# A spectral layer and a mixture of experts on one core: a prefix product in another PSUM ring, bias products over 128 rows, opening loads in another order, and one test for three tiles

## The chip, the cores and the metric

The kernel runs as one program on one core of one Trainium2 chip. The metric is device time in microseconds (us), from one execution of the whole program; a measurement is the median of some such executions. In the profile, PE is TensorE (PEld its weight loads), DVE is VectorE, ACT is ScalarE, POOL is GpSimd, and SP is the engine whose queue issues most DMAs. A "q" behind an engine's name (SPq, POOLq) means its sequencer.

## The reference

Eight sequences of 2496 tokens with 256 channels go through a spectral layer, and all 19968 tokens of its output through a mixture of eight experts, of which each token uses one:

```python
X = np.fft.rfft(x, axis=1)                       # x: (8, 2496, 256)
Yr = Xr @ w_r - Xi @ w_i + b_r
Yi = Xr @ w_i + Xi @ w_r + b_i
Y = soft_threshold(Yr, 0.01) + 1j * soft_threshold(Yi, 0.01)
y = np.fft.irfft(Y, n=2496, axis=1).reshape(19968, 256)

expert = argmax(y @ w_gate, axis=1)              # 8 experts
gate = softmax(y @ w_gate)[expert]
out = gate * (relu(y @ w1[expert]) @ w2[expert]) # 256 -> 1024 -> 256
```

## The kernel before

**The spectral part.** The transform of 2496 = 39 x 64 points is done in two stages of matmuls. For a batch `b`, `fwd_a` multiplies 39-point pieces of `x` (product `pa`), and the result goes to DRAM (`spec_dram<-ae`, or `spec_dram<-z` for the first batch). `turn(b, s)` reads it back in another order (`t<-spec_dram`, two DMAs for each step `s` of ten), and `fwd_b` does the 64-point stage with a table `bm` (product `pb`). `halves` splits the result into high and low parts for exact products on DVE and ACT. `mix` multiplies by the weights (products `pk` and `pm`; `pk` is read into `k`, then `pm` and `k` are added to `u`, in the profile `v`), `shrink` is the soft threshold (`y`), and `inv_b` (product `pv`, table `bi`) and `inv_a` (products `pz` and `py`, result `yb`) transform back. One loop of 80 iterations `it`, ten for each batch, holds all of this: iteration `it` does `fwd_b` of the next step, `mix` of its own, `shrink` of the one before and `inv_b` of the one before that, and places pieces of `fwd_a` of a later batch and of `inv_a` of an earlier one by lists of offsets. For the last batch the two halves of `pm` begin with a product of the tiles `ones` and `bias_r`, which adds `b_r` and `b_i` (row 0 of `bias_r` holds the rounded bias, row 32 what rounding left; both tiles have 33 rows).

**PSUM.** The accumulators lie in small rings of banks. Pool `psi` has a ring `u` of four banks (`pa`, `pv`, `pz`, the experts' `po`, some of the first iteration's) and a ring `yo` of two banks (`py`, and small products of routing and of the tables). Pool `psf` has one bank `b` (`pb`) and one bank `m` (`pk`, then `pm`); a product that takes a bank waits until its last tenant has been read.

**Routing.** For each half batch `route` finds the expert of every token and its place among that expert's rows. The places need a prefix sum over 117 partitions, which is the small product `pr` (lines 668 to 670, two matmuls), read by DVE into `rb`. POOL then scatters the rows into `xs_dram`. `route` and `table` are generators: `tick(n)` lets the oldest of them take `n` steps, each a small DVE operation or two, between the other work. `write_blank` fills eight blank tiles of `xs_dram` by eight DMAs from POOL.

**The experts.** Tiles of 256 rows are multiplied with `w1` (`ph`, line 949; ACT makes `hh`, DVE `hl`) and `w2` (`po`, lines 983 to 986); POOL scatters the results to `out`. `table(0)` and `table(1)` compute which expert and rows each tile has. `finish_last` runs `table(1)` beside the first seven tiles; it ends with the products `pq` and `pl`, whose input `lap` DVE writes. 85 tiles are possible; `experts_rest` runs tiles 7 to 81 always, and 82 to 84 each under a test (`tc.If`) of a count `live`. With these inputs none of the three is run.

The order on PE, SP, ACT and DVE is the order in which the code is written; on SP, DMAs stand in one queue.

Of the kernel before, what the change touches and what calls it, by code (L numbers as in the profile page):

```python
# [24 lines left out]
D = 256  # L25
# [75 lines left out]
class Kernel:  # L101
# [71 lines left out]
    def open_forward(self, st):  # L173
# [18 lines left out]
        self.bias_r = f.tile([33, 2, D], F32R, name="bias_r")  # L192
        self.ones = f.tile([33, 128], F32R, name="ones")
# [67 lines left out]
    def split_bias(self, part):  # L261
        nc = self.nc
        if part == 0:
            nc.scalar.activation(self.bias_r[0:32], self.bias[0:32], AF.Copy, scale=self.tcol[0:32, 2:3])
        elif part == 1:
            bh = self.w.tile([33, 2, D], F32R, tag="y", name="bh", bufs=3)
            nc.scalar.copy(bh[32:33], self.bias[32:33])
            nc.vector.tensor_sub(self.bias_r[32:33], self.bias[32:33], bh[32:33])
        else:
            nc.scalar.activation(self.ones, self.ident[0:33], AF.Copy, scale=0.0, bias=1.0)  # L270
# [75 lines left out]
    def mix(self, b, s):  # L346
# [25 lines left out]
        if b or s:  # L372
            p = self.psf.tile([128, 2, D], F32, tag="m", name="pm", bufs=1)
        else:
            p = self.psi.tile([128, 512], F32, tag="u", name="pm", bufs=4).rearrange("p (a d) -> p a d", a=2)
# [67 lines left out]
    def spectral(self, fwd):  # L443
# [7 lines left out]
        for i, pair in enumerate(pairs):  # L451
            self.fwd_a(0, *pair)
            if i == 4:
                self.load_basis("bm", 0, 2)
                self.load_w("r")
            if i == 6:
                self.load_w("i")
                for h, v in ((0, self.b_r), (1, self.b_i)):
                    self.nc.sync.dma_start(self.brow[:, h, :], bass.AP(v.tensor, v.offset, [[D, 1], [1, D]]))
        self.turn(0, 0)  # L460
        self.turn(0, 1)
        self.load_basis("bm", 2, 6)
        self.turn(0, 2)
        if nb > 1:
            self.load_x(1, 0)
        self.turn(0, 3)
        self.load_basis("bi", 0, 4)
# [9 lines left out]
        for b in range(1, nb):  # L477
            at = 10 * b - 10
            for i, o in enumerate((1, 2, 2, 3, 3, 4, 4, 5, 5, 6, 6) if b == 1 else (-3, -2, -1, 0, 0, 1, 2, 3, 4, 5, 6)):
                first[at + o].append((b, *pairs[i]))  # L480
            for q, o in enumerate((None, 0, 1, 2, 3, 4) if b == 1 else (-7, -5, -4, -2, 0, 2)):
                if o is not None:
                    loads[at + o].append((b, q))
# [9 lines left out]
        for it in range(n):  # L493
# [35 lines left out]
            for a in pieces[it][1:]:  # L529
                self.inv_a(*a)  # L530
            for a in loads[it]:
                self.load_x(*a)
# [4 lines left out]
            if it == 6:  # L537
                self.write_blank(self.us[b, s][0:1, 0, 0:1])
            if it < 4:
                self.load_basis(*(("bm", 6, 12), ("bi", 4, 10), ("bm", 12, 20), ("bi", 10, 20))[it])  # L540
            if it + 4 < n and (it != 6 or nb == 1):
# [48 lines left out]
    def breathe(self):  # L590
        self.tick(3)

    def finish_last(self):
        tiles = itertools.chain.from_iterable(self.step(t) for t in range(BUSY))
        fill = itertools.chain(self.first1(), self.first2())
        for i in range(GH + 1):
# [14 lines left out]
        self.jobs.append(self.table(1))  # L611
        for _ in tiles:
            self.breathe()
# [7 lines left out]
    def route(self, b, hf, y):  # L621
# [46 lines left out]
        p = self.psi.tile([128, 512], F32, tag="yo", name="pr")  # L668
# [36 lines left out]
    def table(self, last):  # L705
# [82 lines left out]
        if last:  # L788
            lap = rt.tile([128, 128], F32, name="lap")
            nc.vector.tensor_copy(lap, fin[:, 3:4].broadcast_to((128, 128)))  # L790
            for _ in range(4):
# [226 lines left out]
    def experts_rest(self, late):  # L1018
        late.enter_context(self.tc.manual_schedule(engines={mybir.EngineType.Activation, mybir.EngineType.DVE}))
        main = self.nt - RARE  # L1020
# [3 lines left out]
        live = self.nc.values_load(self.tabs[1][0:1, 3, 0:1], min_val=0, max_val=self.nt)  # L1024
        nt = self.nt
        for t in range(main, nt):
            with self.tc.If(live > t - self.early):
# [30 lines left out]
```

## Time and profile before

| | |
|---|---|
| median of 3 runs | 1551.67 us (1549.34 to 1552.24) |
| the profiled execution's own time | 1549.26 us |
| its span, first to last instruction | 1547.4 us |
| PE busy | 1512.6 us, 98% of the span |
| DVE, ACT, POOL busy | 62%, 49%, 25% |
| mean granted TensorE clock | 0.995 |

The span falls into an opening (0 to 35 us), the loop of 80 iterations (35 to about 570 us), a stretch in which the last batch is transformed back and the first expert tiles run (to about 670 us), and the experts. A busy PE in these tables includes the time in which a matmul runs through the array behind the next one, so that the steady spacing of starts tells more than the busy time.

### The profile page before, as it was taken

What the parts mean: (1) busy time and instruction counts of PE and PEld (TensorE: products, weight loads), DVE (VectorE), ACT (ScalarE), POOL (GpSimd) and SP (SyncE); (2) the same over time, 40 slices, a digit from 0 to 9 for tenths busy, and PEclk for the clock granted to TensorE, in tenths of its full rate; (3) what the DMA queues carried; (4) which work ended last, traced back from release to release, by engine and by line L of the source; (5) the groups of instructions that cost most, each with busy time, mean ns of one, the idle gap of its engine ahead of it and who ended that gap; (6) DMA issues with size and microseconds to landing.
All of it is one profiled execution on the core that took longest, in us unless ns stands there. A gap on an engine that the chain in (4) does not pass through costs nothing. (4 is left out here: it accounts for less than half of the span.)

```text
span 1547.4 us, 35414 instructions
## 1 busy us (share of the span) xinstructions
PE 1512.6 (98%) x10808; PEld 1383.2 (89%) x10808; DVE 957.2 (62%) x2178; ACT 759.0 (49%) x1629; POOL 392.5 (25%) x550
## 2 busy tenths in 40 slices
PE   8999999999999999999999999999999999999997
PEld 3779899999898889899999999999999999999996
DVE  3778888889898777745555455454545445445442
ACT  2666766767666565434444434343434334334332
POOL 1100243343444453333421111111111111111111
PEclk9999999999999999999999999999999999999999
DMA  7954455555543332434443323232314124132210
GB/s 227 269 177 115 132 169 149 151 165 153 156 143 118 108 78 54 114 90 104 120 115 97 99 53 93 56 94 64 85 42 105 43 50 100 43 82 65 50 42 20
DMA packets 194726, 162.03 MB, mean 105 GB/s; under 512 B 127868, under 2 KB 164516, under 8 KB 194513
## 3 DMA queue, kind: packets, MB, share of 16 engines
q1 hardware_dynamic: 174705, 115.53, 29.2%
q0 software_dynamic: 19808, 44.03, 8.4%
q8 instruction: 88, 1.44, 0.4%
q14 instruction: 125, 1.02, 0.2%
HBM read 241.99 MB, written 66.37 MB: 199 GB/s over the span
## 5 line engine op out<-in xcount | busy, mean ns | idle before, releaser
L986 PE MATMUL po<-h,hh 128*128 128x512 f32 x1312 | 461.9, 395 | 0.0
L949 PE MATMUL ph<-xh,h 128*128 128x256 f32 x1312 | 372.0, 284 | 1.1 <-DVE hl L955 1.0
L949 PE MATMUL ph<-xl,h 128*128 128x256 f32 x1312 | 371.1, 283 | 0.0
L949 PE MATMUL ph<-xh,l 128*128 128x256 f32 x1312 | 370.7, 283 | 0.0
L983 PE MATMUL po<-h,hl 128*128 128x256 f32 x1148 | 323.9, 282 | 0.0
L955 DVE SCALAR_TENSOR_TENSOR hl<-ph,hh 128x512 fp32r<-128x512 f32 x328 | 226.1, 689 | 147.4 <-ACT hh L954 95.0
L954 ACT ACTIVATE hh<-ph 128x512 fp32r<-128x512 f32 x328 | 193.7, 598 | 205.5 <-PE ph L949 197.8
L986 PEld LDWEIGHTS po<-h,hh 128*128 128x128 f32 x1312 | 241.5, 188 | 43.4
L995 POOL DMA_INDIRECT out<-o,row x124 | 123.2, 994 | 581.6 <-DVE o L993 479.0
L993 DVE SCALAR_TENSOR_TENSOR o<-po,xr,part 128x256 f32<-128x256 f32 x156 | 75.4, 484 | 302.3 <-ACTq L911 153.7
L949 PEld LDWEIGHTS ph<-xh,l 128*128 128x128 f32 x1312 | 251.2, 191 | 3.7
L949 PEld LDWEIGHTS ph<-xh,h 128*128 128x128 f32 x1312 | 251.2, 191 | 2.5 <-DVE hl L955 2.1
L949 PEld LDWEIGHTS ph<-xl,h 128*128 128x128 f32 x1312 | 251.2, 191 | 0.0
L992 ACT ACTIVATE part<-po,xr 128x256 f32<-128x256 f32 x156 | 73.8, 473 | 334.5 <-PE po L986 318.3
L983 PEld LDWEIGHTS po<-h,hl 128*128 128x128 f32 x1148 | 215.5, 188 | 6.0 <-DVE hl L955 1.6
L690 POOL DMA_INDIRECT xs_dram<-yb,pos x176 | 179.8, 1021 | 103.5 <-issue 55.8
L392 DVE SCALAR_TENSOR_TENSOR y<-v,r 64x256 f32<-64x256 f32 x320 | 133.4, 417 | 5.0 <-ACT r L386 0.8
L421 PEld LDWEIGHTS pz<-iw,z 128*120 128x120 f32 x704 | 90.7, 183 | 22.2 <-issue 22.1
L421 PE MATMUL pz<-iw,z 128*120 128x136 f32 x704 | 96.7, 280 | 0.0
L409 ACT COPY z<-pv 128x256 f32<-128x256 f32 x160 | 92.7, 700 | 2.1 <-PE pa L293 1.4
L326 PE MATMUL pb<-bm,t 128*128 128x128 f32 x640 | 85.4, 276 | 5.1 <-DMA t<-spec_dram 2.8
L337 ACT COPY re<-pb 128x256 f32<-128x256 f32 x80 | 29.6, 370 | 116.8 <-PE pb L326 102.7
(183 smaller groups left out, 2556.7 us busy)
## 6 DMA issues: line engine op xcount, KB each, us to landing
r<-moe_w SPq DMA_DIRECT2D x672, 128.0 KB
r<-moe_w SPq DMA_DIRECT2D x166, 512.0 KB
xq<-xs_dram SPq DMA_DIRECT2D x332, 64.0 KB
t<-spec_dram SPq DMA_DIRECT2D x160, 128.0 KB
spec_dram<-ae SPq DMA_DIRECT2D x78, 240.0 KB
x<-x SPq DMA_DIRECT2D x40, 384.0 KB
x<-x SPq DMA_DIRECT2D x40, 84.0 KB
xs_dram<-yb,pos POOLq DMA_INDIRECT x176
```

What stands on the lines that cost most here:

```text
L326: nc.tensor.matmul(p[:, c, :, kp, :], t[:, kp, c * 128:(c + 1) * 128], self.bm[:, 2 * s + kp, :], start=True, stop=True)
L392: nc.vector.scalar_tensor_tensor(out=y[q * 64:q * 64 + 64, kp, :], in0=u[h, q, :], scalar=LAM, in1=r[h, q, :], op0=ALU.add, op1=ALU.min)
L409: nc.scalar.copy(self.zs[b % 2][:, c, 0:NB, 4 * s:4 * s + 4].rearrange("p n a -> p a n"), p[:, c].rearrange("p a r n -> p (a r) n"))
L421: nc.tensor.matmul(p[:120, c * 136:(c + 1) * 136], self.zs[b % 2][:, c, 3 * g:3 * g + 3, :].rearrange("p j a -> p (j a)"), self.iw[:, c, : ...
L690: i = nc.gpsimd.indirect_dma_start(out=self.xs[:, :], out_offset=bass.IndirectOffsetOnAxis(ap=pos[:n, g:g + 1], axis=0), in_=y[:n, g, 0:XW ...
L949: nc.tensor.matmul(p[:, i, :], a[:, c, f * 128:(f + 1) * 128], v[:, c, :], start=m == 0, stop=m == 5)
L954: nc.scalar.activation(hh[:, s, :], p, AF.Relu)
L955: nc.vector.scalar_tensor_tensor(out=hl[:, s, :], in0=p, scalar=0.0, in1=hh[:, s, :], op0=ALU.max, op1=ALU.subtract)
L983: nc.tensor.matmul(p[:, :D], hl[:, f - 1, hs], w2[:, f - 1, 0, :], start=False, stop=False)
L986: nc.tensor.matmul(p, hh[:, f, hs], w2[:, f].rearrange("p a d -> p (a d)"), start=f == 0, stop=f == 7)
L993: nc.vector.scalar_tensor_tensor(out=o[:, h, :], in0=p[:, :D], scalar=xr[:, h, 0:1], in1=part, op0=ALU.mult, op1=ALU.add)
L995: i = nc.gpsimd.indirect_dma_start(out=self.out[:, :], out_offset=bass.IndirectOffsetOnAxis(ap=at[h], axis=0), in_=o[:, h, :], in_offset=N ...
```

## The change

Five groups of edits.

- `route`'s product `pr` takes a bank of the ring `u` (four) in place of `yo` (two).
- `ones` and `bias_r` have 128 rows in place of 33, the added rows of `bias_r` being zero; the bias matmuls are over 128 rows.
- The opening loads `bm` 0:4 at once (0:2 before), then 4:8 (2:6 before), and reads `turn(0, 3)` and `bi` ahead of the first `x` of batch 1. In the first iterations each load of `bm` or `bi` stands ahead of the `x` loads of that iteration. `pm` of step 1 takes a bank of `u`, as that of step 0 does, and the first `fwd_a` of batch 1 stands an iteration later. `write_blank` is called in iteration 11 in place of 6.
- While only `table(1)` is left, `breathe` gives it two steps in place of three, and it waits seven steps in place of four between `lap` and `pl`.
- `live` is read ahead of tile 7, and one test stands around the three conditional tiles. In SP's, PE's, ACT's and DVE's order the read moves from behind the last tile to the place ahead of tile 7; on POOL it stays at the end.

```diff
-        self.bias_r = f.tile([33, 2, D], F32R, name="bias_r")
-        self.ones = f.tile([33, 128], F32R, name="ones")
+        self.bias_r = f.tile([128, 2, D], F32R, name="bias_r")
+        self.ones = f.tile([128, 128], F32R, name="ones")
...
-            nc.scalar.activation(self.bias_r[0:32], self.bias[0:32], AF.Copy, scale=self.tcol[0:32, 2:3])
+            nc.scalar.activation(self.bias_r, self.bias, AF.Copy, scale=self.tcol[:, 2:3])
...
-            nc.scalar.activation(self.ones, self.ident[0:33], AF.Copy, scale=0.0, bias=1.0)
+            nc.scalar.activation(self.ones, self.ident, AF.Copy, scale=0.0, bias=1.0)
...
-        if b or s:
+        if b or s > 1:
             p = self.psf.tile([128, 2, D], F32, tag="m", name="pm", bufs=1)
         else:
             p = self.psi.tile([128, 512], F32, tag="u", name="pm", bufs=4).rearrange("p (a d) -> p a d", a=2)
...
-                self.load_basis("bm", 0, 2)
+                self.load_basis("bm", 0, 4)
...
-        self.load_basis("bm", 2, 6)
+        self.load_basis("bm", 4, 8)
         self.turn(0, 2)
+        self.turn(0, 3)
+        self.load_basis("bi", 0, 4)
         if nb > 1:
             self.load_x(1, 0)
-        self.turn(0, 3)
-        self.load_basis("bi", 0, 4)
...
-            for i, o in enumerate((1, 2, 2, 3, 3, 4, 4, 5, 5, 6, 6) if b == 1 else (-3, -2, -1, 0, 0, 1, 2, 3, 4, 5, 6)):
+            for i, o in enumerate((2, 2, 3, 3, 4, 4, 5, 5, 5, 6, 6) if b == 1 else (-3, -2, -1, 0, 0, 1, 2, 3, 4, 5, 6)):
...
+            if it < 4:
+                self.load_basis(*(("bm", 8, 12), ("bi", 4, 10), ("bm", 12, 20), ("bi", 10, 20))[it])
+            if not it:
+                self.turn(*todo[4])
             for a in loads[it]:
                 self.load_x(*a)
...
-            if it == 6:
+            if it == 11:
                 self.write_blank(self.us[b, s][0:1, 0, 0:1])
-            if it < 4:
-                self.load_basis(*(("bm", 6, 12), ("bi", 4, 10), ("bm", 12, 20), ("bi", 10, 20))[it])
-            if it + 4 < n and (it != 6 or nb == 1):
+            if 0 < it < n - 4 and (it != 6 or nb == 1):
...
-        self.tick(3)
+        self.tick(2 if len(self.jobs) == 1 and self.last_table else 3)
...
-        p = self.psi.tile([128, 512], F32, tag="yo", name="pr")
+        p = self.psi.tile([128, 512], F32, tag="u", name="pr", bufs=4)
...
-            for _ in range(4):
+            for _ in range(7):
                 yield
             p = self.psi.tile([128, 512], F32, tag="yo", name="pl")
...
-        main = self.nt - RARE
+        main, nt = self.nt - RARE, self.nt
+        live = self.nc.values_load(self.tabs[1][0:1, 3, 0:1], min_val=0, max_val=nt)
         for t in range(BUSY, main):
             for _ in self.step(t):
                 pass
-        live = self.nc.values_load(self.tabs[1][0:1, 3, 0:1], min_val=0, max_val=self.nt)
-        nt = self.nt
-        for t in range(main, nt):
-            with self.tc.If(live > t - self.early):
+        with self.tc.If(live > main - self.early):
+            for t in range(main, nt):
                 if t > main:
                     self.nt = t
                     self.weights_now(t)
```

On SP's queue, behind the reads `turn(0, 0)` and `turn(0, 1)` of the opening, stood before (`bm<-c_bm 128x512` is 256 KB, `128x768` 384 KB; `x<-x` of 96 rows 384 KB; each `t` 128 KB twice):

```order
L216 DMA bm<-c_bm 128x512
L313 DMA t_243<-spec_dram 64x2x256 x2
L286 DMA x<-x 96x1x1024
L286 DMA x<-x 21x1x1024
L313 DMA t_249<-spec_dram 64x2x256 x2
L216 DMA bi<-c_bi 128x512
L286 DMA x<-x 96x1x1024
L286 DMA x<-x 21x1x1024
L216 DMA bm<-c_bm 128x768
```

And now, at the same place:

```order
L216 DMA bm<-c_bm 128x512
L313 DMA t_243<-spec_dram 64x2x256 x2
L313 DMA t_246<-spec_dram 64x2x256 x2
L216 DMA bi<-c_bi 128x512
L286 DMA x<-x 96x1x1024
L286 DMA x<-x 21x1x1024
L216 DMA bm<-c_bm 128x512
```

The first row was `bm` 2:6 and is now 4:8; `turn(0, 3)` (`t_249` before, `t_246` now) has moved ahead of the first `x` of batch 1; `bm` 6:8, which stood in the last row of before behind two loads of `x`, is now in the first.

On DVE, beside the fourth expert tile that `table(1)` runs along with, stood before, from the tile's first `hl` to its second (the small 128x8 operations are `table(1)`'s):

```order
L955 SCALAR_TENSOR_TENSOR hl<-ph,hh 128x512
L921 STREAM_TRANSPOSE xf<-xq 128x8x2x32
L741 TENSOR_TENSOR st_9430<-pfb,cnt 128x8
L744 TENSOR_TENSOR te<-tcol,pfb 128x8
L746 COPY ge<-te 128x8
L747 TENSOR_REDUCE fin<-te 128x1
L744 TENSOR_TENSOR te<-tcol,pfb 128x8
L747 TENSOR_REDUCE fin<-te 128x1
L749 TENSOR_SCALAR fin<-fin 128x2
L750 TENSOR_TENSOR fin<-fin 128x1
L955 SCALAR_TENSOR_TENSOR hl<-ph,hh 128x512
```

And now, between the same two:

```order
L959 SCALAR_TENSOR_TENSOR hl<-ph,hh 128x512
L925 STREAM_TRANSPOSE xf<-xq 128x8x2x32
L742 TENSOR_TENSOR cnt<-cnt,used 128x8
L718 COPY pfa<-cnt 128x8
L721 COPY pfb<-pfa 128x1
L722 TENSOR_TENSOR pfb<-pfa 128x7
L959 SCALAR_TENSOR_TENSOR hl<-ph,hh 128x512
```

Eight small operations stood between the two, now four, and the rest of the table has moved to later places; `pq` and `pl` stand on PE about a tile later than before.

On POOL, at the end of the program, behind the read of `live` (the row `ISA` is the instruction that, where a tile is skipped, counts up the semaphores of its DMAs; the profile calls it INC_SWDGE_SEM), stood before:

```order
L1027 COMPARE_AND_BRANCH
L911 UNCONDITIONAL_BRANCH
L995 DMA out<-o,row 19968x256 x2
L1027 UNCONDITIONAL_BRANCH
L1027 ISA
L1027 UNCONDITIONAL_BRANCH
L1027 COMPARE_AND_BRANCH
L903 UNCONDITIONAL_BRANCH
L911 UNCONDITIONAL_BRANCH
L995 DMA out<-o,row 19968x256 x2
L1027 UNCONDITIONAL_BRANCH
L1027 ISA
```

and the same once more for the third tile. Now stands there, for all three tiles:

```order
L1029 COMPARE_AND_BRANCH
L915 UNCONDITIONAL_BRANCH
L999 DMA out<-o,row 19968x256 x2
L907 UNCONDITIONAL_BRANCH
L915 UNCONDITIONAL_BRANCH
L999 DMA out<-o,row 19968x256 x2
L907 UNCONDITIONAL_BRANCH
L915 UNCONDITIONAL_BRANCH
L999 DMA out<-o,row 19968x256 x2
L1029 UNCONDITIONAL_BRANCH
L1029 ISA
```

A program that skips the tiles met three compares and three `ISA`, and now meets one of each.

## Rows read from the trace of the kernel before

**Rows 1.** PE's waits over the span: us in total, times, longest.

```profile
PE py L438 <- ACT yb L439: 7.7, 11, 1.3
PE pb L326 <- DMA t<-spec_dram: 2.8, 2, 2.0
```

**Rows 2.** Three stretches: us, each engine's busy us (x instructions), clock, DMA share, GB/s.

```profile
50.00:75.00 25.00, 24.82 (x165) 20.05 (x164) 19.95 (x45) 17.78 (x39) 2.67 (x7) 1.00 0.95 277
100.00:125.00 25.00, 25.00 (x196) 23.02 (x195) 19.92 (x44) 18.05 (x45) 0.00 (x0) 1.00 0.37 106
...
580.60:584.00 3.40, 3.24 (x15) 2.90 (x15) 3.26 (x12) 3.05 (x9) 1.87 (x4) 0.50 0.24 73
```

**Rows 3.** Timeline, 30 to 43 us: start, us, engine, what [idle before <-releaser].

```profile
32.62 1.13 PE L326 MATMUL pb<-bm,t 128*128 128x128 f32 x8 [1.12 <-DMA bm<-c_bm]
...
37.09 0.44 SPq L216 DMA_DIRECT2D bm<-c_bm  x1
...
37.55 1.02 PE L293 MATMUL pa<-x,far 117*120 117x512 f32 x2
...
39.66 0.39 PE L359 MATMUL pm<-whd,sh 128*128 128x256 f32 x1 [1.09 <-DVE k L368]
...
41.72 0.69 DVE L379 TENSOR_TENSOR v<-pm,k 128x512 f32<-128x512 f32 x1
...
42.52 1.13 PE L326 MATMUL pb<-bm,t 128*128 128x128 f32 x8 [1.18 <-DMA spec_dram<-ae]
```

**Rows 4.** Timeline, 73 to 84 us, POOL, SP and PE.

```profile
73.09 4.27 POOL L232 DMA_DIRECT2D xs_dram<-blank  x8 [0.45 <-POOL blank L230]
...
75.71 5.79 SPq L313 DMA_DIRECT2D t<-spec_dram  x4
...
83.55 1.13 PE L326 MATMUL pb<-bm,t 128*128 128x128 f32 x8 [2.04 <-DMA t<-spec_dram]
```

**Rows 5.** Timeline of PE and DVE around three of the products pr.

```profile
190.85 0.20 PE L670 MATMUL pr<-carry_b,ones_b 117*117 117x8 bf16 x1
...
192.16 0.29 PE L438 MATMUL py<-zl,gh 120*117 120x272 f32 x1
192.93 0.39 PE L438 MATMUL py<-zh,gh 120*117 120x272 f32 x1 [0.47 <-ACT yb L439]
...
193.26 0.17 DVE L672 SCALAR_TENSOR_TENSOR rb<-pr,base 117x8 f32<-117x8 f32 x1
193.28 0.29 PE L438 MATMUL py<-zl,gh 120*117 120x272 f32 x1
193.40 0.29 PE L359 MATMUL pm<-whd,sh 128*128 128x256 f32 x1
...
530.08 0.38 PE L438 MATMUL py<-zh,gh 120*117 120x272 f32 x1 [1.18 <-ACT yb L439]
...
590.24 0.38 PE L438 MATMUL py<-zh,gh 120*117 120x272 f32 x1 [0.61 <-ACT yb L439]
```

**Rows 6.** The bias products: the line's group, and PE's timeline around one.

```profile
L355 PE MATMUL pm<-bias_r,ones x20: 378/381/384, 501.7 to 564.8; 33*128 33x256 f32 x20
...
553.17 0.28 PE L359 MATMUL pm<-whd,sl 128*128 128x256 f32 x1
553.38 0.38 PE L355 MATMUL pm<-bias_r,ones 33*128 33x256 f32 x1
553.69 0.39 PE L359 MATMUL pm<-whs,sh 128*128 128x256 f32 x1
```

**Rows 7.** PE's timeline beside the last table.

```profile
637.82 0.39 PE L949 MATMUL ph<-xh,h 128*128 128x256 f32 x1 [0.73 <-DVE hl L955]
...
650.65 0.49 PE L794 MATMUL pl<-ident,lap 128*128 128x128 f32 x2 [1.50 <-DVE lap L790]
```

**Rows 8.** The end on POOL: two lines' groups (ns min/median/max, first and last start).

```profile
L1027 POOLq INC_SWDGE_SEM  x3: 1180/1194/1236, 1538.1 to 1541.0; - x3
...
L1054 POOLq DRAIN  x3: 46/109/4317, 1542.3 to 1547.1; - x3
```

More of the change, by code (lines that the diff above doesn't have):

```diff
@@ L595, in finish_last @@
         fill = itertools.chain(self.first1(), self.first2())
+        self.last_table = False
         for i in range(GH + 1):
@@ L611, in finish_last @@
         self.jobs.append(self.table(1))
+        self.last_table = True
         for _ in tiles:
```

## The prediction

> **What bounds the kernel now.** I read the table first: PE is busy for 98% of the span, at a granted clock of 0.995. So no other engine is a bound over any long stretch, and an edit can gain only where PE stands still, where its matmuls are spaced wider than they need be, or behind its last matmul. Next I read PE's waits. There the reader is to see how little there is: the longest entry is `py` waiting for ACT's copy `yb`, 7.7 us in eleven waits, then `pb` waiting for the reads of `spec_dram`, 2.8 us [rows 1]. The remaining views are timelines at those places, to see what the waiting product's bank or input hangs on, and the stretches, for the DMA load. Between 50 and 75 us the DMA engines are 0.95 busy at 277 GB/s, and 50 us later 0.37 at 106 GB/s [rows 2]. Waits alone don't tell all: the twenty bias products cause hardly a wait but break the spacing of matmuls [rows 6], and the end of the program has no PE in it at all [rows 8].
>
> **The change part by part.** All sums are against the profiled execution's own 1549.26 us.
>
> *Opening loads and `pm` of step 1.* The larger first load puts 128 KB more into a saturated queue ahead of everything that the first `pb` needs: at 277 GB/s [rows 2] that is 0.47 us lost. Three waits of PE are addressed: 1.12 us for `bm` at 32.62, 1.09 us for `k` at 39.66, and 1.18 us at 42.52 [rows 3]. The last is put down to a write of `spec_dram`, but that `pb` is step 3's, which reads `bm` 6:8, and these came with the load issued at 37.09 [rows 3]; I take that load as its cause. What is late next is DVE: beside these steps it works without a break, and `v` of step 1 starts at 41.72 behind the four `y` that step 0's `pv` needs [rows 3]. So `pv` can start at about 41.75, where before it stood behind a `pb` begun at 42.52, about 1.0 us later (an estimate from that row's 1.13), so at 43.5. That gives 1.75, of which one `pa`, 1.02 us with its run-out [rows 3] and so some 0.9 of PE's time, is only moved to a later iteration. The first wait I count at nothing: the `pk` behind it needs `halves` of step 0 on ACT and DVE. Sum: 1.75 - 0.9 - 0.47 = 0.4 us gained. Bounds: 0.5 lost, if none of the waits comes back, and 2.9 gained, if all three (3.39) do. I take the inner value because DVE's row is the one that binds.
>
> *`write_blank` five iterations later.* POOL's eight writes start at 73.09; SP's four reads `t`, of which the first two feed the first step of batch 1, are issued from 75.71 on and take until 81.5 to issue; PE waits 2.04 us for them at 83.55 [rows 4]. Eight writes of 264 KB are 2.1 MB, which at 277 GB/s [rows 2] is 7.6 us, so from 73.1 to 80.7: they and the reads share the engines. Without them the reads' 256 KB need about 1 us behind 75.7 and some latency, well ahead of 81.5. Gain 2.0. At the new place, near 100 us, the engines are 0.37 busy [rows 2] and steps are read some three iterations ahead, which hides the writes; if that cover were too thin, the wait of 2.0 would stand there again. Bounds 0 and 2.2.
>
> *`pr` in the ring `u`.* At 190.85 `pr` takes one of the two banks of `yo`, and DVE reads it only at 193.26. The second `py` of the next pair therefore starts 0.77 us behind the last matmul of the first (192.16 to 192.93), waiting for `yb`, where matmuls else follow each other by 0.12 (193.28 to 193.40) [rows 5]. That is 0.64 lost. Five products `pr` have a like wait (the one shown, and near 261, 330, 398 and 468 us). Two more stand at 530.08 and 590.24, with 1.18 and 0.61 idle [rows 5], which with the same 0.17 of refilling are 1.35 and 0.78. Together 3.2 + 2.1 = 5.3 us; the other waits of [rows 1] do not follow a `pr`, and stay. In `u` the product holds one of four banks for the same 2.4 us, in which PE takes two banks for `pz`; the older tenants of these have to be read by then. I take off 0.3 for this: 5.0. Bounds 0 (the wait moves to a `pz`) and 5.3.
>
> *Bias products over 128 rows.* Each of the twenty starts 0.21 us behind its forerunner (553.17 to 553.38), and its follower 0.31 us behind it (to 553.69) [rows 6]; 256 columns else take 0.12 [rows 5]. So each costs 0.09 + 0.19 = 0.28 us more than a product over 128 rows beside it, and twenty cost 5.6. A few begin `pm` behind a wait for `k` which hides the 0.09, and the iterations of the last batch become shorter, so that ACT and DVE may be late now and then: 5.2. Bounds 0 and 5.7. The two ACT operations that fill the tiles have the same number of columns as before, and stand once, off PE's path.
> The rows show a matmul that costs more with fewer rows. The Trainium skill says otherwise ("TensorE: Matmul & The Clock Gate", section "Why this matters for your kernels"): a single matmul over 32 rows takes the same time as one over 128. By that rule this edit gives nothing and the sum below is 11.7. The Trainium skill's page "TensorEngine Tiling (Array Packing)", under "Key Properties", says that a change of tiling mode drains TensorE, with which the rows' gaps on both sides agree.
>
> *The last table.* PE waits 0.73 us at 637.82 for an `hl` that stands on DVE behind eight small operations of the table, and 1.50 us at 650.65 for `lap` [rows 7]. Four small operations now stand there, so I take half of the first, 0.4. `pl` now comes when `lap` is long done, but the `ph` that stood behind it needs an `hl` which DVE makes at the same time: two thirds, 1.0. Together 1.4; bounds 0 and 2.2.
>
> *One test for three tiles.* POOL ends the program. Behind its last scatter three INC_SWDGE_SEM of 1.2 us stand in a row, their starts 1538.1 to 1541.0, so 1.45 us for each with its compare; a DRAIN of 4.32 us from 1542.3 follows [rows 8]. Two of the three go: 2.9 us. The DRAIN starts with the last of them done. If it waits for a moment that does not hang on them, the gain is 0; if its 4.3 us is three times 1.44, a share for each, it shrinks too, and the gain is 5.8. Nothing in the rows favours either end; I take 2.9. The read of `live` on PE and SP ahead of tile 7 costs nothing while their sequencers run ahead of the data path.
>
> Sum: 0.4 + 2.0 + 5.0 + 5.2 + 1.4 + 2.9 = 16.9 us. 1549.26 - 16.9 = 1532.4 for an execution like the profiled one. That one lies 2.4 below the median of the three runs, whose spread is 2.9; a median of the changed kernel should lie between, so I add half of it, 1.2: **1533.5**.
>
> **The rivals.**
>
> *The bias products' gaps have nothing to do with their rows.* Each is the first of its sum and brings a new pair of operands; were that the price, 128 rows would change nothing. For it: the gap does stand at the head of a sum. Against it: the `pm` at 193.40 is also the first of its sum and follows by 0.12 [rows 5]. Saving 16.9 - 5.2 = 11.7, time 1538.7. The Trainium skill's rule on few rows, cited above, leads to the same.
>
> *The ring `u` gives the wait back.* Between `pr` and `rb` two `pz` and later `pv` and `pa` take banks, and one bank fewer turns round. If each of the seven waits comes back there: saving 11.9, time 1538.5. For it: ACT and DVE, which empty these banks, are 18 to 20 of 25 us busy [rows 2]. Against it: they have four banks' time, 5 to 6 us, to do so.
>
> *The waits on DMA and the end go nowhere.* The reads of the opening wait for the next load, and the DRAIN ends when it did: 0.4, 2.0 and 2.9 fall away; saving 11.6, time 1538.8.
>
> *Slower.* All sixteen `pr` make PE wait until DVE has read them, up to 2.4 us each [rows 5], because the bank is wanted before. The other terms save 11.9; to end 3.1 above the time before, these waits must cost 15.0, so from 0.95 us for each product on, and at 2.4 each the time would be 1549.26 + 1.2 + 26.5 = 1577. Against it: PE takes four more banks of `u` only in most of an iteration, longer than 2.4 us.
>
> **How the numbers follow.** The forecast has 0.64; the three rivals on one term 0.10 each; two of them at once 0.03 (about 1544, still faster); the slower one 0.03. 0.2% of this time, 3.1 us, is about what a measurement can tell from no change. All cases but the last are faster by more, apart from some of the double one: faster 0.94, same 0.03, slower 0.03. The range goes down to 1528, where most of the upper bounds (24.1 at their sum) would be met in part, or where the half clock from 580.6 to 584.0 [rows 2] goes too (up to 1.7 us, which I count at nothing since the waits around it stay); up to 1541, which takes in each single rival.
>
> **What would show it.** Right: no wait of `py` behind a `pr`; spacing of 0.12 on both sides of the bias products; no `pb` waiting near 82 us; one INC_SWDGE_SEM, and a DRAIN as long as before; no wait of `pl`; `pb` of step 3 about 1.5 us earlier than 42.5. Wrong: `pz` or `pv` waiting for a bank behind `pr`; bias products still at 0.21 and 0.31; a `t` waited for near 100 us; a DRAIN that has grown by what the others lost.

## Result and profile after

The changed kernel takes 1533.38 us (median of four runs, 1532.36 to 1534.23) where the kernel before takes 1551.36 in runs on the same chip: a ratio of 0.9888, 95% interval 0.9873 to 0.9903, so 18.0 us or 1.1% faster. The profiled execution has a span of 1530.9 us, 16.5 less than before, and took 1532.63 with what lies around the span. The forecast was 1533.5 for the median, and 1532.4 for an execution like the profiled one.

PE's waits over the span (what waits <- what it waits for; us in total, times, longest):

```profile
PE py L438 <- ACT yb L439: 3.5, 4, 1.3
...
PE ph L953 <- DVE hl L959: 2.0, 2, 1.8
...
PE pm L355 <- ACT k L366: 1.2, 2, 0.7
```

`py` for `yb` has gone from eleven waits and 7.7 us [rows 1] to four and 3.5; `pb` for the reads `t` is out of the list. Two waits have grown: `ph` for `hl` (1.0 us before), and the bias products' `pm` for `k` (0.8 before).

Around a product `pr`, on PE and DVE, and around a bias product (with the group of its line):

```profile
188.40 0.20 PE L674 MATMUL pr<-carry_b,ones_b 117*117 117x8 bf16 x1
...
189.70 0.29 PE L438 MATMUL py<-zl,gh 120*117 120x272 f32 x1
189.83 0.29 PE L438 MATMUL py<-zh,gh 120*117 120x272 f32 x1
...
190.81 0.17 DVE L676 SCALAR_TENSOR_TENSOR rb<-pr,base 117x8 f32<-117x8 f32 x1
```

```profile
L355 PE MATMUL pm<-bias_r,ones x20: 278/283/388, 495.5 to 553.2; 128*128 128x256 f32 x20
...
541.35 0.28 PE L359 MATMUL pm<-whd,sl 128*128 128x256 f32 x1
541.47 0.28 PE L355 MATMUL pm<-bias_r,ones 128*128 128x256 f32 x1
541.59 0.28 PE L359 MATMUL pm<-whs,sh 128*128 128x256 f32 x1
```

DVE still reads `pr` 2.4 us behind it, but the second `py` now follows the first pair by 0.13 and not by 0.77 [rows 5]. The bias product stands 0.12 behind its forerunner and 0.12 ahead of its follower (0.21 and 0.31 in [rows 6]), and its own median is 283 ns where it was 381.

The blank, on SP, PE and POOL, and two stretches (us, busy us of PE, PEld, DVE, ACT, POOL, clock, DMA share, GB/s):

```profile
75.62 2.58 SPq L313 DMA_DIRECT2D t<-spec_dram  x4
...
81.26 1.05 PE L326 MATMUL pb<-bm,t 128*128 128x128 f32 x8
...
99.93 4.26 POOL L232 DMA_DIRECT2D xs_dram<-blank  x8 [0.45 <-POOL blank L230]
```

```profile
100.00:125.00 25.00, 25.00 (x196) 23.02 (x195) 20.63 (x45) 17.19 (x43) 4.19 (x8) 1.00 0.61 192
...
568.00:590.00 22.00, 21.31 (x170) 20.60 (x169) 17.89 (x55) 16.76 (x44) 9.06 (x14) 1.00 0.20 53
```

The four reads are issued in 2.58 us instead of 5.79, and `pb` starts 2.29 us sooner, without a wait [rows 4]. The writes now run where DMA was 0.37 busy and is 0.61, and PE has no gap there. The products that ran at the lower clock level before, from 580.6 us on (0.50) [rows 2], now start some 12 us earlier, at about 568, and run at the full level (1.00 in the second stretch shown).

The opening on PE, the last table on DVE and PE, and two groups of the end on POOL:

```profile
23.96 2.03 PE L240 MATMUL pbias<-first,first 1*128 1x512 f32 x2 [2.10 <-DMA first<-b_i]
...
31.78 1.95 PE L326 MATMUL pb<-bm,t 128*128 128x128 f32 x16
...
40.33 1.13 PE L326 MATMUL pb<-bm,t 128*128 128x128 f32 x8
...
42.96 0.71 PE L405 MATMUL pv<-bi,y 128*128 128x128 f32 x4 [0.61 <-DVE y L392]
```

```profile
632.17 2.50 DVE L902 TENSOR_TENSOR h<-r,h 128x512 fp32r<-128x512 f32 x4
...
634.59 0.68 DVE L959 SCALAR_TENSOR_TENSOR hl<-ph,hh 128x512 fp32r<-128x512 f32 x1
...
635.33 0.38 PE L953 MATMUL ph<-xh,h 128*128 128x256 f32 x1 [1.75 <-DVE hl L959]
```

```profile
L1029 POOLq INC_SWDGE_SEM  x1: 1237/1237/1237, 1524.4 to 1524.4; - x1
...
L1057 POOLq DRAIN  x3: 46/109/4317, 1525.7 to 1530.6; - x3
```

Step 3's `pb` is 2.2 us sooner than in [rows 3], although the first `pb` comes 1.4 later. In this profile that first `pb` waits for no load: it stands right behind the filling products `pw` of the opening, and from 24.0 to 30.8 us the clock was 0.50. Both waits of [rows 7] are gone, and one of 1.75 us stands in their place. At the end one INC_SWDGE_SEM is left of three, and the long DRAIN is as long as before [rows 8].

To see where the 16.5 us come from I matched PE's products in order and took, for each, its start before less its start after: PE's lead. What a stretch gives is the growth of the lead. (Step 8 is the last step of the opening batch ahead of the blank's wait, at 76.1 us before; the other columns are times of before too.)

| kernel | step 8 | 84.5 | 112 | 497 | 568 | 589 | 620 | 671 | last `po` |
|---|---|---|---|---|---|---|---|---|---|
| after | 0.08 | 2.37 | 2.39 | 6.09 | 11.98 | 12.83 | 13.71 | 13.93 | 13.81 |
| u_pr | 1.21 | 3.50 | 3.53 | 3.49 | 7.99 | 8.83 | 8.94 | 9.18 | 9.16 |
| u_bias33 | 1.20 | 3.48 | 3.49 | 7.21 | 8.60 | 8.84 | 9.66 | 9.88 | 9.82 |
| u_blank6 | 1.23 | 1.16 | 0.00 | 3.63 | 9.48 | 10.33 | 11.15 | 11.38 | 11.36 |
| u_open | -0.57 | 1.72 | 1.75 | 5.44 | 11.29 | 12.10 | 12.33 | 12.53 | 12.53 |
| u_table | -1.18 | 1.11 | 1.13 | 4.82 | 10.67 | 11.52 | 12.37 | 12.36 | 12.25 |
| same_again | 1.06 | 3.35 | 3.38 | 6.98 | 12.85 | 12.87 | 13.75 | 12.73 | 12.67 |
| spread | 0.61 | 2.90 | 2.92 | 6.51 | 12.38 | 13.21 | 14.06 | 15.50 | 15.33 |
| open2_spread | 2.02 | 4.31 | 4.34 | 8.19 | 14.07 | 14.92 | 15.75 | 17.19 | 17.18 |

The remaining 2.7 us of the span lie behind the last `po`. The first column matters for all that follows: kernels whose opening is the same program differ there by up to 2.4 us (-1.18 to 1.23), so a part's worth is read from the stretch in which it lies and not from the span.

### The profile page after: what moved, and what is told of

It reads as the page before. It is cut to its first block, busy times and chain, and to the rows that moved or that the text cites. A ratio compares the mean times of both kernels' runs of the same rounds, so it can differ in the third digit from the quotient of the medians.

```text
span 1530.9 us, 35408 instructions
## 1 busy us (share of the span) xinstructions
PE 1504.4 (98%) x10808; PEld 1380.3 (90%) x10808; DVE 955.3 (62%) x2178; ACT 758.9 (50%) x1629; POOL 392.6 (26%) x550
## 3 DMA queue, kind: packets, MB, share of 16 engines
q8 instruction: 88, 1.44, 0.4%
## 5 line engine op out<-in xcount | busy, mean ns | idle before, releaser
L405 PE MATMUL pv<-bi,y 128*128 128x128 f32 x640 | 85.1, 276 | 1.2 <-DVE y L392 0.8
```

The source lines that it names most:

```text
L405: nc.tensor.matmul(p[:, c, kp, :, :], y[:, kp, c * 128:(c + 1) * 128], self.bi[:, 2 * s + kp, :], start=True, stop=True)
```

## Experiments

The first six each undo one part of the change; medians are compared with the 1533.4 of the changed kernel, ratios with the kernel before in the same series (1550.3 to 1550.5, where it was 1551.36 beside the changed kernel). With four runs each, and series that differ by 1 us, medians alone settle no difference of 1 to 2 us. Labels are those of the table.

**u_pr: the prefix product in the banks `yo` again.**

```diff
-        p = self.psi.tile([128, 512], F32, tag="u", name="pr", bufs=4)
+        p = self.psi.tile([128, 512], F32, tag="yo", name="pr")
```

> The changed kernel with only pr put back into the ring yo. If pr's hold on one of two banks made the seven waits of py, they come back, each on the second py of the next pair: five of 0.64 us of spacing in the loop, one of about 1.3 and one of about 0.8; the span is 5.3 to 6.0 us above 1530.9, and the steps of the loop between 110 and 500 us fall behind by 0.7 for each half batch, 3.7 in all. If the ring u had mostly given the wait back elsewhere, the span is up by 0 to 2 us.

Measured 1538.03 us (1537.33 to 1539.68), ratio 0.9923 (0.9907 to 0.9940). PE's timeline of this kernel:

```profile
188.65 0.29 PE L438 MATMUL py<-zl,gh 120*117 120x272 f32 x1
189.42 0.39 PE L438 MATMUL py<-zh,gh 120*117 120x272 f32 x1 [0.47 <-ACT yb L439]
189.64 0.28 PE L438 MATMUL py<-zh,gl 120*117 120x272 f32 x1
```

The wait is back, and the lead does not grow between 112 and 497 us, where it grew by 3.70. The spacing is 0.77 instead of 0.13, and the next one 0.22 instead of 0.12: the matmul that starts after a stop takes longer and holds up its follower by another 0.10. So each of the five costs 0.74; with 1.39 in the last batch and 0.77 behind 589 this part is worth 5.9 us. The span is only 4.6 longer, less than expected, because the opening of this profile came out 1.1 us ahead.

**u_bias33 and bias65: how many rows.** The bias products over 33 rows as before, and over 65 rows (the same two lines with 65 in place of 33).

```diff
-        self.bias_r = f.tile([128, 2, D], F32R, name="bias_r")
-        self.ones = f.tile([128, 128], F32R, name="ones")
+        self.bias_r = f.tile([33, 2, D], F32R, name="bias_r")
+        self.ones = f.tile([33, 128], F32R, name="ones")
...
```

> The changed kernel with ones and bias_r of 33 rows again. If few rows are what widens the spacing, the twenty products again start 0.21 us behind their forerunner, their follower 0.31 behind them and the one after that 0.22 behind (0.12 each over 128 rows), which is 0.39 us for each and 7.8 for twenty; but in the last batch waits for v and k on the bank m, about 3.4 us longer now than before the change, shrink again, so the span is 4 to 5 us above 1530.9. If row count does not matter, as a page states, spacing and span stay as in the changed kernel, within 0.5 us.

> The changed kernel with 65 rows in ones and bias_r in place of 128, which leaves the sums as they are. If the price hangs on the operands' being short of the full array (any number under 128), spacing is 0.21, 0.31 and 0.22 us as with 33 rows and the span 4 to 5 us above 1530.9. If it hangs on the matmul using half of the array's rows or fewer, 65 rows run like 128: spacing 0.12 on all sides, span 1530.9 within 0.5 us.

Over 33 rows: 1536.67 us (1536.61 to 1536.92), ratio 0.9911 (0.9895 to 0.9928). Over 65: one run of 1533.70. PE's timelines of the two, 33 rows first:

```profile
544.50 0.28 PE L359 MATMUL pm<-whd,sl 128*128 128x256 f32 x1
544.71 0.38 PE L355 MATMUL pm<-bias_r,ones 33*128 33x256 f32 x1
545.02 0.39 PE L359 MATMUL pm<-whs,sh 128*128 128x256 f32 x1
545.25 0.28 PE L359 MATMUL pm<-wls,sh 128*128 128x256 f32 x1
```

```profile
541.78 0.28 PE L359 MATMUL pm<-whd,sl 128*128 128x256 f32 x1
541.91 0.28 PE L355 MATMUL pm<-bias_r,ones 65*128 65x256 f32 x1
542.02 0.29 PE L359 MATMUL pm<-whs,sh 128*128 128x256 f32 x1
```

Place, operands' order and columns are the same; only the rows differ, and 65 rows behave like 128. So the gaps are due to the product's 33 rows (the rival that blamed the head of a sum falls), and there are three: 0.21, 0.31 and 0.23 where 0.12 stands else, 0.39 us for each product, 7.8 for twenty. The lead from 497 to 568 us grows by 5.89 in the changed kernel, by 5.83 with 65 rows and by 1.39 with 33, so 128 rows are worth 4.5 and not 7.8. (The spans are 4.0 and 1.1 us longer than the changed kernel's. With 33 rows the opening came out 1.1 us ahead, and 0.6 went into a stretch at clock 0.50 near 571 us; with 65, 0.7 into a longer wait of `ph` for `hl` at 599 us (1.13 instead of 0.28), far from the bias products.) Where the other 3.3 are shows when the spacings are compared product by product. The spacings at the bias products give 7.3, since two of the twenty start behind a wait for `k` in either kernel, which hides part of their gap; and five stops in front of `pk` and `pm` are longer with 128 rows, by 2.9 together. Of PE's waits between 490 and 570 us, these lines differ, in the changed kernel and with 33 rows:

```profile
PE pm L355 <- ACT k L366: 1.2, 2, 0.7
PE pk L359 <- DVE v L379: 0.8, 1, 0.8
PE pk L359 <- DVE carry L679: 0.6, 1, 0.6
PE pk L359 <- issue: 0.6, 1, 0.6
```

```profile
PE pm L355 <- ACT k L366: 0.8, 2, 0.5
PE pk L359 <- ACT sh L338: 0.2, 1, 0.2
```

**u_blank6: the blank at iteration 6 again.**

```diff
-            if it == 11:
+            if it == 6:
```

> The changed kernel with write_blank in iteration 6 again. If POOL's eight writes delay the first reads of batch 1, PE waits about 2 us at the ninth step near 81 us and the span is 2.0 to 2.4 us above 1530.9. If the new order of the opening loads had removed that wait by itself, the step comes at 81.3 as now and the span moves by less than 0.5 us.

Measured 1535.31 us (1535.09 to 1536.86), ratio 0.9905 (0.9889 to 0.9922). PE's timeline and two stretches of this kernel, and one of the kernel before:

```profile
82.39 1.13 PE L326 MATMUL pb<-bm,t 128*128 128x128 f32 x8 [2.12 <-DMA t<-spec_dram]
```

```profile
79.50:83.40 3.90, 1.77 (x16) 1.60 (x15) 2.46 (x5) 0.38 (x1) 0.00 (x0) 1.00 0.91 298
83.50:86.90 3.40, 3.40 (x16) 3.02 (x15) 1.48 (x3) 2.90 (x6) 0.00 (x0) 0.50 0.59 176
```

```profile
80.60:84.50 3.90, 1.86 (x16) 1.68 (x15) 2.59 (x5) 0.51 (x1) 0.00 (x0) 1.00 0.95 314
```

The wait is back and costs 2.3 of the lead. Behind it, here and not in the kernel before, the granted clock was 0.50 (1.2 of 2.4 GHz) for 3.4 us, which cost 1.2 more. In the 3.9 us ahead, 79.5 to 83.4, PE had been busy for 1.77; in the kernel before it was busy for 1.86 of 3.9 at the same place, and the clock did not fall behind it. So a stop of 2 us may or may not be followed by a stretch at the lower level. That the span came out 2.5 longer, close to the expectation, is in part luck: the 1.2 is offset by an opening that was 1.15 ahead.

**u_tail: a test of its own for each of the three conditional tiles.**

```diff
-        with self.tc.If(live > main - self.early):
-            for t in range(main, nt):
+        for t in range(main, nt):
+            with self.tc.If(live > t - self.early):
...
```

The read of `live` stands behind the last tile again, as before the change.

> The changed kernel with live read behind the last tile again and three tests. If the counting instruction of each skipped tile is what costs, three INC_SWDGE_SEM stand in a row behind the last scatter, the DRAIN behind them still takes 4.3 us, and the span is 2.7 to 3.0 us above 1530.9. If the DRAIN hung on how many of them there are, it would differ from 4.32 us; if the early read of live had cost something ahead of tile 7, that would come back as a gain of up to 0.5 us in the starts of the tiles.

Measured 1535.64 us (1534.68 to 1537.04), ratio 0.9906 (0.9889 to 0.9922). The last `po` comes within 0.02 us of that of the changed kernel, the span ends 2.8 later, with a DRAIN of 4.32 us as before:

```profile
L1031 POOLq INC_SWDGE_SEM  x3: 1180/1194/1236, 1524.3 to 1527.3; - x3
```

**u_open: the old loads and order of the opening.** It puts back loads of two and four slices of `bm`, the old places of step 3 and of the later loads, `pm` of step 1 in bank `m`, and the first `fwd_a` of batch 1 an iteration earlier.

```diff
-                self.load_basis("bm", 0, 4)
+                self.load_basis("bm", 0, 2)
...
-        self.load_basis("bm", 4, 8)
+        self.load_basis("bm", 2, 6)
...
```

> The changed kernel with the opening as before: order and sizes of the first loads, pm of step 1 in the bank m, the first pa of batch 1 an iteration earlier; write_blank stays late. If the opening's gains and losses cancel, as the steps at 76 us say (76.1 before, 76.0 now), the first pb starts 1.4 us earlier than the 31.8 of the changed kernel, step 3 about 2 us later than its 40.3, and the span is 1530.9 within 0.5 us. If the new order of loads is what made the room for batch 1, the ninth step waits again near 81 us and the span is 2 us longer.

Measured 1534.57 us (1531.74 to 1535.38), ratio 0.9891 (0.9874 to 0.9907). The difference of 1.2 lies within the spread of the runs. In the profile the first `pb` starts at 30.20, as expected, and step 3 at 43.15, some 0.8 later than expected, behind a wait of 1.93 us. From step 8 to 84.5 us the lead grows by 2.29, as in the changed kernel: the late blank needs no help from the new order of loads. The span is 1.3 longer, more than expected; half of it is the opening and half a longer wait of `ph` for `hl` at 599 us (1.10 instead of 0.28).

**u_table: the old pacing of the last table.**

```diff
-        self.tick(2 if len(self.jobs) == 1 and self.last_table else 3)
+        self.tick(3)
...
-            for _ in range(7):
+            for _ in range(4):
```

> Undoes the pacing of the last table alone (three pieces of work at every breath again, pl four pauses behind lap instead of seven). Theory: the two waits that were removed, 0.73 us before an hl and 1.50 us before lap, came back in the changed kernel as one wait of 1.91 us in the spacing (633.29 to 635.33, ph for hl), because hl stands on DVE behind the four operations of a weight split; with the old pacing the two waits return, that one goes, and the median is 0 to 0.8 us above the 1533.4 of the changed kernel. Rival (the size that the prediction gave): 1.4 slower, 1534.8, with the 1.91 us still there beside the two.

Measured 1533.11 us (1531.44 to 1534.19), ratio 0.9885 (0.9866 to 0.9904). PE's timeline of this kernel, beside the table:

```profile
625.45 0.38 PE L953 MATMUL ph<-xh,h 128*128 128x256 f32 x1 [0.73 <-DVE hl L959]
...
638.30 0.49 PE L798 MATMUL pl<-ident,lap 128*128 128x128 f32 x2 [1.52 <-DVE lap L794]
```

Its products `pq` and the `hl` behind the weight split, and `pq` in the changed kernel:

```profile
632.69 1.03 PE L788 MATMUL pq<-ident,fin 128*1 128x128 f32 x8
...
636.50 0.69 DVE L959 SCALAR_TENSOR_TENSOR hl<-ph,hh 128x512 fp32r<-128x512 f32 x1
```

```profile
641.42 1.03 PE L788 MATMUL pq<-ident,fin 128*1 128x128 f32 x8
```

Both old waits are back, the wait for `hl` behind the weight split is gone from the list. Two things had covered it. The `hl` is done at 637.19, when PE has no product left since 636.6, so without `pl` the next `ph` would wait some 0.6 us for it. And eight products `pq` stand on PE just ahead of the tile; in the changed kernel they come at 641.42, a tile later. There PE needs 2.73 us instead of 3.89 from the last `po` ahead of the tile to the last `ph` ahead of the wait, while `hl` comes only 0.13 later behind that `po`. From step 8 to 671 us the lead grows by 13.54 here and by 13.85 in the changed kernel: this part is worth 0.3 us. The medians (1533.1 and 1533.4) do not show it.

**same_again: the changed kernel once more.**

> The changed kernel itself, word for word. Theory: its opening differs from execution to execution, with the length of the half clock before the first pb, so that this pb starts anywhere from 30.0 to 32.1 us (31.78 in the profile of the changed kernel) and the span moves with it; median 1533.4 within 1.0, and step 8's stage up to 1.8 us earlier than in the profile of the changed kernel. Rival: the opening is a fixed property of the order of loads; the first pb starts at 31.8 within 0.2.

Measured 1533.79 us (1531.17 to 1533.86), ratio 0.9887 (0.9867 to 0.9908). Its first `pb` starts at 30.51, not 31.78, and its lead at step 8 is 1.06: the opening is no fixed property of the order of loads. Later it loses 0.8 and 1.2 against the changed kernel's profile in two places, by two stretches at the lower clock that the profile of the changed kernel does not have (568 to 590 and 629 to 645 us; both 1.00 there):

```profile
568.00:590.00 22.00, 21.80 (x163) 21.02 (x162) 17.27 (x53) 15.92 (x41) 8.30 (x14) 0.93 0.20 53
629.00:645.00 16.00, 14.25 (x90) 12.78 (x89) 10.60 (x28) 5.93 (x11) 5.37 (x7) 0.89 0.24 64
```

With the lead of 12.9 added, the first of the two stands where the kernel before had its own (567.8 here, 580.6 there).

**spread: half of tile 4's weight split behind its second `hl`.**

```diff
-        if t:
+        if t == 4:
+            with self.changed(t):
+                for q in range(2):
+                    self.part2(q)
+        elif t:
             self.split2(t)
...
+            if t == 4 and f2 == 1:
+                with self.changed(t):
+                    for q in range(2, 4):
+                        self.part2(q)
+                self.weights(t + 1, 2)
             next(work, None)
```

> The changed kernel with the second-layer weight split of tile 4 in two halves, the first ahead of the tile's first hl as before, the second behind the second hl; nothing else. Theory: the 1.91 us of spacing at 633.29 (ph for hl) is DVE's 2.50 us of weight split ahead of hl; with half of it there hl starts about 1.25 us sooner, the wait shrinks to 0.5 to 0.9 us, and the kernel is about 1.0 us faster than the changed one (1532.4 by the medians), if the second half is done before the third hl is wanted. Rival: hl is late because of the ReLU copies on ACT and the table's small operations; the wait stays at 1.6 to 1.9 us and the time at 1533.4.

Measured 1531.68 us (1531.12 to 1532.04), ratio 0.9880 (0.9862 to 0.9898). DVE and PE in its timeline:

```profile
631.80 1.29 DVE L902 TENSOR_TENSOR h<-r,h 128x512 fp32r<-128x512 f32 x2
...
633.75 0.39 PE L957 MATMUL ph<-xh,h 128*128 128x256 f32 x1 [0.55 <-DVE hl L963]
```

The idle time falls from 1.75 to 0.55, and the lead grows by 1.44 from 620 to 671 us instead of 0.22. What held `hl` was the split in front of it on DVE. The runs overlap with those of same_again (1531.17 to 1533.86), so the gain is the 1.2 us of the trace rather than the 1.7 of the medians.

**pm_u_last: `pm` of the last batch in the ring of four.** The question was whether the new waits of the last batch come from the one bank `m`.

```diff
-        if b or s > 1:
+        if not last and (b or s > 1):
```

> The changed kernel with pm of the last batch in the ring u in place of the bank m that it shares with pk. If the waits of the last batch (pk for v, pm for k; at 505.9, 510.3, 544.0, 549.9 and 551.4 us, 4.3 us in all) come from the one bank, they go and the span is 2.5 to 4 us below 1530.9. If ACT and DVE are simply late there, or the ring u with pz, pv, pr and pm in four banks makes pz or pv wait, the span moves by less than 1 us or grows.

Measured 1533.62 us (1531.33 to 1534.78), ratio 0.9884 (0.9867 to 0.9900): no gain. Its waits of the last batch:

```profile
PE pz L421 <- DVE zl L427: 1.4, 1, 1.4
PE pv L405 <- DVE zl L427: 1.3, 1, 1.3
```

The waits for `k` and `v` are gone, so it was at the one bank that PE stood. But waits for `zl`, and one of 0.7 for `y`, have come in their place, and from 497 to 589 us the lead grows by 6.33 instead of 6.74. So the bank alone is not what costs the time. (This profile also has a stretch at clock 0.50 near 637 us, so its span says nothing.)

**open2 and open2_spread: two versions that might beat both.** The first loads of the second filter half and of `bm` go behind the writes of `spec_dram`, the biases ahead of the first half, and 30 instead of 16 filling products `pw` stand in front of the first `pb`; then the same with the split in halves.

```diff
             if i == 4:
-                self.load_basis("bm", 0, 4)
-                self.load_w("r")
-            if i == 6:
-                self.load_w("i")
...
+                self.load_w("r")
+        self.load_w("i")
+        self.load_basis("bm", 0, 4)
...
-        self.keep_warm(16)
+        self.keep_warm(30)
```

> The changed kernel with w_i and the first bm loaded behind the first batch's writes to spec_dram in place of among them, the two bias vectors ahead of w_r, and 30 warm-up products in place of 16 behind the product of the bias. If the first pb is late because 512 KB stand in the queue ahead of its rows, and the half clock comes from the idle time ahead of the product of the bias, the reads of spec_dram are issued 1.5 to 2 us earlier, the clock stays at its upper level, the first pb starts at 28.5 to 30 in place of 31.8, and the span is 1 to 2.5 us below 1530.9. Rival: the weights then come late, DVE and ACT split them later, the first pk starts no earlier than 34.7, and the span stays within 0.5 us or is longer.

> Both of the above steps that gained or should: opening loads in the order of the kernel with w_i and the first bm behind the writes of spec_dram (1531.5 in its run), and the weight split of tile 4 in halves. Theory: the gains add, since that opening gave back 1.0 us in the same wait for hl; 1529.5 to 1530.5, and no wait of ph for hl over 0.9 us near 632. Rival: the wait goes elsewhere in the tiles that follow, and it stays at 1531.5.

open2 took 1531.52 us (1530.71 to 1533.52), ratio 0.9876 (0.9859 to 0.9892); open2_spread 1530.40 (1529.26 to 1530.50), ratio 0.9871 (0.9853 to 0.9889), the fastest here. PE at the opening of open2:

```profile
21.51 1.12 PE L240 MATMUL pbias<-first,first 1*128 1x512 f32 x2
...
29.88 1.13 PE L326 MATMUL pb<-bm,t 128*128 128x128 f32 x8 [0.67 <-DMA t<-spec_dram]
```

`pbias` no longer waits for `b_i`, and there is no stretch at the lower clock before the first `pb`. Both were changed at once, so which of them counts is not shown. In open2 alone part of the opening's gain went into a longer wait for `hl` at tile 4 (2.71 us idle; the lead falls by 0.7 from 620 to 671 us, where it grew by 0.2 in the changed kernel); with the split in halves that wait is 0.55 and the gain stays.

## Why the prediction was right, and where its terms were off

The median lies 0.1 us from the forecast and the profiled execution 0.2 from its own, but that is closer than the terms are: misses of up to 1.1 us cancel, and two profiles of one program differ by 1.1 (1530.9 and 1532.0). The mechanism held in the blank, `pr`, bias and end parts; in the last table it did not, and the opening is not settled. By part, in us saved:

| part | predicted | measured | from |
|---|---|---|---|
| opening | 0.4 | 0.1; 0.8 in the mean | lead at step 8; all profiles |
| blank | 2.0 | 2.3 | 76 to 84.5; u_blank6 |
| `pr` | 5.0 | 5.9 | u_pr |
| bias products | 5.2 | 4.5 | 497 to 568; u_bias33 |
| half clock at 580 | 0 | 0.85 | 568 to 589 |
| last table | 1.4 | 0.3 | u_table |
| end | 2.9 | 2.7; 2.8 | behind the last `po`; u_tail |

*Opening.* What waits last is as forecast: `pv` of step 0 waits for the `y` (0.61 us idle at 42.96). The first `pb` was priced 0.47 later, and its time is in fact spread widely. Against the same product before, the ten kernels with this opening lie from 2.67 us later to 0.32 earlier, 0.87 later in the mean. Two causes show in their profiles. In three of them, the changed kernel's and two more, that `pb` waits for nothing but stands behind the products `pw`, which ran at clock 0.50 for 6.8 us. In the other seven it waits for `t`, which is read 0.6 us later in the mean than in the two profiles of the old opening (issued at 27.26 and 26.68), near the price. One of the seven, u_tail, has no stretch at the lower level and is late all the same:

```profile
31.66 2.15 PE L326 MATMUL pb<-bm,t 128*128 128x128 f32 x16 [2.19 <-DMA t<-spec_dram]
```

From there to step 8 each of the ten gains 0.9 to 1.5, where the sum had 0.85 (1.75 less 0.9). The old opening too moved by 0.57 between its two profiles. So the term is positive in the mean (the ten have a lead of 0.48 at step 8, the two 0 and -0.57), but no single profile gives its size, and the medians leave it unsettled.

*Blank.* As predicted, in both places: no wait near 82 us, and no gap on PE at the new place.

*`pr`.* Right, and no `pz` or `pv` has a new wait behind a `pr` (one `pv` waits 0.4 us for `zl`, in u_pr too). The step that was off is the price of a stop: I counted to the start of the waiting matmul (0.64) and left out that it holds its follower 0.10 longer. The 0.3 taken off for the ring was not needed.

*Bias.* Two misses nearly cancel. The price of a product left out the third spacing: it is 0.39 and not 0.28, so 7.8 for twenty and not 5.6. And of this, 3.3 did not come. 0.4 was hidden by waits for `k`, as the prediction said of "a few"; the sentence that ACT and DVE "may be late now and then", priced with it at 0.4 in all, took 2.9, in five stops whose idle times sum to 2.2 more than with 33 rows. That these two engines are the reason is argued and not shown: from 497 to 569 us DVE is busy for 58.2 of 72 us and ACT for 49.8, and with another bank for `pm` the waits moved to other work of theirs. The Trainium skill's rule ("TensorE: Matmul & The Clock Gate", section "Why this matters for your kernels") is stated for 32 rows, and no run here has 32; to 33 rows it does not carry over, and the rival that took it so is refuted by u_bias33 and bias65.

*Last table.* This is the step that failed. The first wait went whole, 0.7 instead of the 0.4 predicted. For the second the step assumed that `ph` behind `pl` would find its `hl` with a third of the wait left, a gain of 1.0; it became a loss of 0.5, since 1.75 us of idle time for `hl` stand where 1.50 for `lap` had stood. This `hl` stands behind four operations of a weight split, 2.5 us of DVE. The wait for `lap` had hidden about 0.6 us of it, and the products `pq`, which the new pacing moved a tile later, most of the rest: without them PE reaches this `ph` 1.2 us sooner. The prediction counted nothing for moving `pq`. spread shows the part of the split: with half of it behind `hl`, the wait is a third and the lead 1.2 us larger. What `pq` is worth follows from the two traces; no run moved it alone.

*End.* Each INC_SWDGE_SEM that went saved its 1.2 us and what stood around it, 1.4 in all; the DRAIN did not change.

*Half clock.* The prediction counted nothing for it and put it into the range. It is not the change's alone: same_again runs the same program with two such stretches, one of them at the very place of the kernel before. Of the thirteen profiles behind the change two have one there (same_again and u_bias33); of the kernel before there is one profile, so whether the change makes it rarer stays open. That the forecast came out right although it left this 0.85 out is luck.

Of the rivals, the gaps without regard to rows (1538.7), the ring that gives the wait back (1538.5) and the end and DMA waits that go nowhere (1538.8) are each refuted by a run that undoes the part (of the last, for the blank and the end; its 0.4 for the opening is unsettled); the slower case needed waits behind all `pr`, and there are none.

## What to carry to other kernels

Price a break in PE's stream by all the spacings that differ from the usual one, the one behind the resuming matmul included; waits are listed by idle time alone and understate it. When twenty small gaps of one stage close, ask how busy the engines are that feed it: here, with DVE busy for 58 of 72 us, 2.9 of 7.8 us came back as waits. Before a wait is removed, or work is moved away from in front of an instruction, look at what else that instruction needs, and at the longest operation that stands in front of *that* on its in-order engine; splitting this one group of operations in two gave 1.2 us, pacing the small ones around it 0.3.

## What was not expected of the hardware

A 256-column matmul over 33 rows among products over 128 takes 381 ns instead of 283 and upsets three spacings, 0.39 us in all (u_bias33); over 65 rows it costs nothing (bias65, one run). The granted clock falls to 0.50 for some 3.4 us in different places in executions of one program: none near 570 or 635 us in the profile of the changed kernel, both in the run of same_again. In the opening the first `pb` moves by up to 3 us between profiles of one opening (30.05 to 33.05), with such stretches and with the arrival of its reads, more than the edit there is worth.
